# A linear attention followed by an FFT-convolution gate: x2 in row tiles of 128, narrow column tiles, whole q loads with even and odd rows apart, and a new tail

## The chip, the cores and the metric

The kernel runs on one core of a Trainium2 chip, whose engines are TensorE (PE, with its weight loads shown as PEld), VectorE (DVE), ScalarE (ACT), GpSimd (POOL) and SyncE (SP, which here only issues DMAs). The metric is device time in microseconds (us) of one launch. Of the kernel before, three runs took 252.71, 253.55 and 256.71 us; the median is 253.55 us.

## The reference

There are 8 batches, 8 heads, 576 positions (S), 64 features per head (D) and a model width of 512 (DM). Inputs and output are fp32. Attention is linear, with cosine weights on the positions; its output goes through a gate with a circular convolution over the positions.

```
r    = maximum(x, 0);  phi(x) = concat[r * cos(theta), r * sin(theta)]      # theta = pi/2 * pos / S
kv   = phi(k)^T v;  z = sum_s phi(k)
att  = (phi(q) kv) / (phi(q) z + 1e-6)            # per batch and head
x    = att as (batch, S, 512)
x1, x2, x3 = split(x @ w_proj)                    # w_proj: 512 x 1536
conv = irfft(rfft(x2) * rfft(filter_fft))         # along S
out  = (x1 * conv * x3) @ w_out                   # w_out: 512 x 512
```

## The kernel before, in words

All matmul operands are fp16, sums are in fp32. The 576 positions of a batch are held as 6 groups (t or j) of 96 rows. For each batch b the work has these stages; a name in parentheses is the function, the line that of the row in the profile.

- Loads (`load_qk`): q, k and v of a batch are loaded and turned to fp16 by POOL's DMA queue into tiles of 96 partitions, 8 heads and 6 x 64 elements; four buffers serve q, k and v together. From batch 2 on q comes in three DMAs (lines 131 and 133), because the last three groups have even and odd partitions swapped.
- `emit_phi`: phi of k (tile kp) and of q (tile qp), on DVE; lines 102 and 104 are the helper `tsc`.
- `emit_va` (L142): four ACT copies per batch put v into a tile with a constant column beside it.
- `emit_kv` (L527): 48 matmuls per batch, the product of phi(k) and v.
- `emit_qt`: transposes phi(q) to the tile qpt, of which there is one. For batches 0 and 1 TensorE transposes, with the matrices `ident` and `swap`; from batch 2 on SP issues four transposing DMAs (L539), each over two heads, 12 blocks and all 96 partitions.
- `emit_num` (L568): four pieces (hp) of two heads, each 12 matmuls with weights from qpt, read with a stride of two columns; DVE divides (L574, L577) and writes att (L578).
- `emit_xt` (L617): from batch 2 on, one transposing DMA of 24 blocks turns att into xt.
- `emit_fx` (L595, eviction L610 on ACT): folds att along S into 12 groups of 48 columns, that is 6 pairs of real and imaginary parts for three frequency blocks (bl) of 96 rows.
- `emit_x2` (L634, eviction to x2f L639 on ACT): the x2 third of the projection in frequency. For each of the three blocks and two parts, four matmuls with weights of 96 columns and 512 moving columns: 24 per batch.
- `emit_dft` (L649): the rest of the transform, two matmuls for each block, with the tables tre and tim (96 x 96); ACT evicts (L651), DVE multiplies with the filter's transform h3.
- `emit_gate` (L674): the x1 and x3 thirds, 64 matmuls of 288 columns per batch; ACT evicts (L681, L684), DVE multiplies (g, L699).
- `emit_inv` (L710, L711; L714 on ACT) and `emit_y` (L725 to L730 on DVE): the inverse transform, and its product with g, y.
- `emit_out` (L752): y times w_out in five tiles of 128 rows. The five start at rows 0, 128, 256, 384 and 448, so the last repeats 64 rows of the fourth. ACT evicts to os (L759), in groups of tiles (0,1), (2,3), (4); in the last batch DVE does (L102), tile by tile. SP stores the rows (L772), 15 DMAs per batch; in the last batch the odd ones go on ACT's queue, and in the batch before it some on POOL's.

PSUM is one pool of four units with two banks each, which all stages share. The order of the work is written out by hand in the kernel's body and taken up by a scheduler with `behind(mark)`, which holds a piece back until a marked instruction has been issued. In the main loop (b = 1 to 8) x2, dft, gate and inv of batch b are mixed with num and fx of batch b + 1, with phi, qt, va and kv of batch b + 2, and with out of batch b − 1; va and phi of k wait behind marks `x2f` and `att`. SP's queue takes stores, q transposes and xt in the order in which they are issued. A setup phase in the first 60 us computes the tables on DVE, ACT and POOL beside batch 0 and 1. There POOL issues the loads of batch 0, w_proj in three pieces, then q, k and v of batch 1, the filter (`filt`) and w_out (`wo`).

## Time and profile before

| what | value |
|---|---|
| median of three runs | 253.55 us |
| the profiled execution | 253.76 us |
| its span in the profile | 252.0 us |
| mean granted TensorE clock | 0.97 |
| DMA packets, bytes | 74926, 37.30 MB |
| stores of out by SP of 96, 64, 32 KB | 64, 22, 23 |
| q load from batch 2 on, three DMAs each: 288 KB, 144 KB, 144 KB | about 6 us each to landing |
| qpt transposes, issue to landing | 7.1 us |
| xt transposes, issue to landing | 7.7 us |

The profile is one execution. Busy time is the union of an engine's instructions; matmuls overlap in the pipeline, so a single matmul's mean (some 380 ns for 512 columns) is longer than the pitch at which they come. The chain of waits goes back from the last instruction to what released it. A table by windows gives the busy time of each engine in a stretch, its granted clock (1.00 is full) and the DMA's share. Some groups of the page, with busy us, mean ns, idle time before them and its releaser:

```profile
L674 PE MATMUL x<-xt,wp 128*128 128x288 f16 x512 | 68.1, 286 | 0.0
L634 PE MATMUL x<-wp,fx 128*96 128x512 f16 x192 | 48.1, 395 | 1.6 <-DVE qpt L553 1.6
L752 PE MATMUL out<-wo,y 128*128 128x512 f16 x160 | 36.0, 379 | 0.1
L639 ACT ACTIVATE x2f<-x 96x1024 f16<-96x1024 f32 x24 | 24.5, 1020 | 14.2 <-PE x L634 13.9
L142 ACT COPY va<-vraw 96x768 f16<-96x768 f16 x32 | 25.2, 831 | 9.2 <-DMA vraw<-in_v_dram 9.2
```

128*96 is the weights' shape (rows by columns), 128x512 that of the moving operand.

### The profile page before, as it was taken

The numbers are of one execution on the slowest core, as the hardware profiler recorded it, in microseconds if no ns is written. First come the engines' busy times: TensorE is split into PE (matmuls) and PEld (weight loads), VectorE is DVE, ScalarE is ACT, GpSimd is POOL, SyncE is SP. The second block draws the span as 40 slices with busy tenths as digits, with TensorE's granted clock in tenths as the row PEclk, the third lists the DMA queues.
The fourth block names the chain that finished last, engine by engine and source line by source line (L and its number), as shares of the span: only waits on it lengthen the run. The fifth ranks groups of instructions, "written<-read, shape, count | busy, mean of one in ns | idle before, by whom it ended". The sixth has DMA issues, their size and how long they took to land.

```text
span 252.0 us, 6140 instructions
## 1 busy us (share of the span) xinstructions
PE 226.1 (90%) x2313; PEld 159.9 (63%) x2313; DVE 210.4 (83%) x732; ACT 186.2 (74%) x281; POOL 38.1 (15%) x65
## 2 busy tenths in 40 slices
PE   0197897998988999999999999999999999999980
PEld 0067575655676867686768676867686778557730
DVE  7689899699779999999799979997998595828880
ACT  2244789799797876987698769876987488767720
POOL 8714211501501031103110311000000000000030
PEclk9997998899799999999999999999999999999996
DMA  5999999799999969999999999999982512153054
GB/s 68 167 205 205 207 200 153 101 166 196 173 121 157 169 56 202 174 176 194 200 225 143 141 217 199 137 183 156 161 197 53 153 41 58 44 146 83 3 153 140
DMA packets 74926, 37.30 MB, mean 148 GB/s; under 512 B 54288, under 2 KB 70160, under 8 KB 74896
## 3 DMA queue, kind: packets, MB, share of 16 engines
q0 software_dynamic: 26176, 17.21, 51.3%
q1 hardware_dynamic: 48320, 19.11, 40.6%
q10 hardware_dynamic: 400, 0.59, 0.7%
q8 instruction: 18, 0.29, 0.5%
q14 instruction: 12, 0.10, 0.2%
HBM read 33.69 MB, written 9.44 MB: 171 GB/s over the span
## 4 chain that ended last, share of the span: by engine, by line
PE 73%; DVE 13%; ACT 7%; DMA 3%; issue 1%; POOL 1%; POOLq 0%; DVEq 0%; ACTq 0%
PE x L674 21%; PE x L634 17%; PE out L752 12%; PE kv L527 5%; PE num L568 4%; PE fx L595 4%; PE dft L649 3%; DMA vraw<-in_v_dram 3%; PE inv L711 2%; PE inv L710 2%; DVE kp L104 2%; ACT va L142 1%; DVE eo L725 1%; DVE att L578 1%; PE qt L547 1%
## 5 line engine op out<-in xcount | busy, mean ns | idle before, releaser
L674 PE MATMUL x<-xt,wp 128*128 128x288 f16 x512 | 68.1, 286 | 0.0
L674 PEld LDWEIGHTS <-wp 128*128 128x128 f16 x512 | 48.9, 98 | 13.9 <-issue 0.9
L634 PE MATMUL x<-wp,fx 128*96 128x512 f16 x192 | 48.1, 395 | 1.6 <-DVE qpt L553 1.6
L752 PE MATMUL out<-wo,y 128*128 128x512 f16 x160 | 36.0, 379 | 0.1
L639 ACT ACTIVATE x2f<-x 96x1024 f16<-96x1024 f32 x24 | 24.5, 1020 | 14.2 <-PE x L634 13.9
L634 PEld LDWEIGHTS <-fx 128*96 128x96 f16 x192 | 23.0, 127 | 16.7 <-issue 3.7
L142 ACT COPY va<-vraw 96x768 f16<-96x768 f16 x32 | 25.2, 831 | 9.2 <-DMA vraw<-in_v_dram 9.2
L578 DVE TENSOR_TENSOR att<-num,rcp 96x768 f16<-96x768 f32 x32 | 30.3, 948 | 0.2
L752 PEld LDWEIGHTS <-y 128*128 128x128 f16 x160 | 15.3, 97 | 17.7 <-DVE y L730 0.6
L527 PE MATMUL kv<-va,kp 96*128 96x65 f16 x384 | 16.6, 199 | 10.2 <-ACT va L142 8.4
L684 ACT CAST x3s<-x 128x576 f16<-128x576 f32 x32 | 20.5, 641 | 5.9 <-PE x L674 5.9
L759 ACT ACTIVATE os<-out 128x1024 f32<-128x1024 f32 (+1 forms) x21 | 17.7, 880 | 9.0 <-PE out L752 8.7
L610 ACT CAST fx<-fx 128x576 f16<-128x576 f32 x32 | 20.6, 645 | 4.9 <-PE fx L595 4.9
L651 ACT CAST xf<-dft 96x1024 f16<-96x1024 f32 x24 | 24.2, 1008 | 0.0
L527 PEld LDWEIGHTS <-kp 96*128 96x128 f16 x384 | 15.1, 101 | 13.6 <-DVE kp L104 11.3
L699 DVE TENSOR_TENSOR g<-x3s,x1s 128x288 f16<-128x288 f16 x64 | 17.2, 299 | 6.8 <-ACT x3s L684 6.8
L681 ACT CAST x1s<-x 128x576 f16<-128x576 f32 x32 | 20.6, 645 | 1.8 <-PE x L674 0.8
L654 DVE TENSOR_TENSOR m<-xf,h 96x1024 f16<-96x1024 f16 x24 | 16.3, 681 | 6.1 <-ACT xf L651 5.1
L568 PEld LDWEIGHTS <-qpt 128*128 128x128 f16 (+1 forms) x384 | 16.2, 103 | 7.7 <-issue 3.9
L725 DVE TENSOR_TENSOR eo<-eq 128x288 f16<-128x288 f16 x64 | 17.5, 297 | 4.4 <-ACT eq L714 4.4
L595 PE MATMUL fx<-fm,att 96*128 96x96 f16 x240 | 17.0, 214 | 3.4 <-DVE att L578 1.7
L595 PEld LDWEIGHTS <-att 96*128 96x128 f16 x240 | 14.3, 101 | 7.6 <-DVE att L578 3.4
(192 smaller groups left out, 409.1 us busy)
## 6 DMA issues: line engine op xcount, KB each, us to landing
out_dram<-os SPq DMA_DIRECT2D x64, 96.0 KB, 2.2
kraw<-in_k_dram POOLq DMA_DIRECT2D x7, 576.0 KB, 8.6
vraw<-in_v_dram POOLq DMA_DIRECT2D x7, 576.0 KB, 8.9
qraw<-in_q_dram POOLq DMA_DIRECT2D x8, 288.0 KB, 6.0
qraw<-in_q_dram POOLq DMA_DIRECT2D x12, 144.0 KB, 5.9
wp<-in_moe_w_proj_dram POOLq DMA_DIRECT2D x3, 512.0 KB, 11.9
out_dram<-os SPq DMA_DIRECT2D x22, 64.0 KB, 2.2
out_dram<-os SPq DMA_DIRECT2D x23, 32.0 KB, 2.1
```

What stands on the lines that cost most here:

```text
L142: nc.scalar.copy(out=va_buf[b % 2][:, hs, :, 0:D], in_=raw_t[(b, "v")][:, hs].rearrange("p h (j d) -> p h j d", j=NJ),)
L527: nc.tensor.matmul(u[:, h // 4, ds((h % 4) * 65, 65)], kp[:, j, h].rearrange("p a b -> p (a b)"), va[:, h, j, 0:65], start=(j == 0), stop= ...
L568: nc.tensor.matmul(u[0:m, hh, ds(t * 65, 65)], qpt[:, c0 : c0 + 2 * m - 1 : 2], kvs[:, h // 4, ds((h % 4) * 65, 65)], start=True, stop=True,)
L578: mark["att", b, hp] = nc.vector.tensor_tensor(out=att[:, :, ds(hp * 128, 128)].rearrange("p t (h d) -> p h t d", h=2), in0=nv[:, :, :, 0: ...
L595: nc.tensor.matmul(dst.rearrange("p (g e o) -> p g e o", e=2, o=8)[:, :, e], att[:, 2 * j + e, ds(c * 128, 128)], fm[0:NP, gs], start=True ...
L610: mark["fx", b] = nc.scalar.copy(out=dst[:, c].rearrange("p g (j o) -> p j g o", j=3), in_=uf[:, 0:768].rearrange("p (j g o) -> p j g o", ...
L634: nc.tensor.matmul(u[0:NP, comp], fx[:, c, ds(comp * 6 + 2 * bl, 2)].rearrange("p a b -> p (a b)"), wp16[:, c, ds(DM, DM)], start=(c == 0) ...
L639: mark["x2f", b, bl] = nc.scalar.mul(out=x2f[:, bl], in_=u[0:NP], mul=X2SC)
L651: mark["xf", b, bl] = nc.scalar.copy(out=xf, in_=u[0:NP])
L674: nc.tensor.matmul(u[:, hf, 0:HS], wp16[:, i, ds(w * DM + c * 128, 128)], xt[:, i, ds(6 * hf, 6)].rearrange("p a b -> p (a b)") if b < DMA ...
L681: mark["x1s", b, c] = nc.scalar.copy(out=x1s, in_=us[0][:, :, 0:HS])
L752: nc.tensor.matmul(u[:, x], y[:, c, ds(OT[t], 128)], wo16[:, c], start=(c == 0), stop=(c == NC - 1),)
```

## The change

- *q.* q gets a buffer of its own, of 112 partitions, and k and v share three buffers. From batch 2 on q comes in two DMAs: even rows to partitions 0 to 47, odd ones to 64 to 111, each partition's whole 6 x 64 elements at once. phi of q then works on 112 partitions, and qp is laid out by halves of the groups. The transposing DMAs are again four, but each takes 48 partitions and 24 blocks (3 groups of all 8 heads). The positions of att's columns stay what the later stages want; num reads qpt without a stride. Some setup columns (`tcol_m`, `ident`, `swap`, `fm`) are computed for the new order.
- *x2.* fx's 576 columns are taken in four row tiles of 128 and one of 64. The last has its four contracted chunks in two halves, of which one goes to PSUM partitions 0 to 63 and one to 64 to 127, alternating. x2f is 128 partitions by five tiles.
- *dft.* A frequency block now lies across row tiles. Seven padded copies of parts of the tables (tpad) are made in the setup, by seven memsets on DVE and eight DMAs on SP, and three of the six sums take two matmuls, so 9 matmuls instead of 6. The last table has its rows twice, which adds the halves of the fifth tile.
- *out.* The fifth tile is 64 rows. Its 512 columns are computed as two halves of 256, one on PSUM partitions 0 to 63 and one on 64 to 127, in alternating matmuls, evicted as 128 x 256 and stored in two halves per piece. Stores cover 48 rows of one residue; SP issues 17 per batch, and POOL none.
- *va.* From batch 4 on two of the four copies are made on DVE, and the marks that hold them back differ.
- *Order.* In the setup the q load of batch 1, the filter and w_out are issued behind phi(0, q). phi of k waits behind mark `att` 3 instead of 1. In the last batches dft 2 and out of batch 6 come ahead of the gates, inv ahead of the third gate, and out of batch 7 starts with tiles 1 and 0, of which three quarters of the contraction come before the last y is needed; tiles 1 and 0 are evicted by DVE, the others half by DVE and half by ACT, and stores alternate between SP and ACT.

```diff
+    tpad = [consts.tile([128, NP], FP16, tag=f"tpad{i}", name=f"tpad{i}") for i in range(7)]
+    q_buf = consts.tile([112, NH, NJ * D], FP16, tag="qraw", name="qraw")
...
-            nc.gpsimd.dma_start(out=rw[:, hs, 0 : 3 * D], in_=view[:, :, 0 : 3 * D])
-            for x in range(2):
-                nc.gpsimd.dma_start(
-                    out=rw[x::2, hs, 3 * D : 6 * D], in_=view[1 - x :: 2, :, 3 * D : 6 * D]
-                )
+            for e in range(2):
+                nc.gpsimd.dma_start(out=rw[ds(64 * e, 48), hs], in_=view[e::2])
...
+        for i, to, tb, bl, lo, n in (
+            (0, 96, tim, 0, 0, 32), (1, 0, tim, 0, 32, 64), (2, 64, tre, 1, 0, 64),
+            (3, 0, tre, 1, 64, 32), (4, 32, tim, 1, 0, 96), (5, 96, tim, 2, 0, 32),
+            (6, 0, tim, 2, 32, 64), (6, 64, tim, 2, 32, 64),
+        ):
+            nc.sync.dma_start(out=tpad[i][to : to + n], in_=tb[lo : lo + n, bl])
...
+            e, half = hp % 2, hp // 2
             nc.sync.dma_start_transpose(
-                out=qpt[:, hsl].rearrange("p h (j n) -> p (h j) n", j=NJ),
-                in_=qp[:, hsl].rearrange("p h j a b -> p (h j a b)"),
+                out=qpt.rearrange("p h (j e m n) -> p (h j) e m n", j=3, e=2, m=2)[:, :, e, half],
+                in_=qp[ds(64 * ((e + half) % 2), 48), half].rearrange("p h j a b -> p (h j a b)"),
             )
...
-                m = NP if hh and t >= 4 else 128
-                c0 = h * S + 2 * NP * (t // 2) + t % 2
+                m = NP if hh and t == NT - 1 else 128
                 nc.tensor.matmul(
-                    u[0:m, hh, ds(t * 65, 65)], qpt[:, c0 : c0 + 2 * m - 1 : 2],
+                    u[0:m, hh, ds(t * 65, 65)], qpt[:, ds(h * S + t * NP, m)],
...
-            for comp in range(2):
-                for c in range(NC):
-                    nc.tensor.matmul(
-                        u[0:NP, comp],
-                        fx[:, c, ds(comp * 6 + 2 * bl, 2)].rearrange("p a b -> p (a b)"),
-                        wp16[:, c, ds(DM, DM)], start=(c == 0), stop=(c == NC - 1),
-                    )
-            mark["x2f", b, bl] = nc.scalar.mul(out=x2f[:, bl], in_=u[0:NP], mul=X2SC)
+            if bl < 2:
+                for x in range(2):
+                    for c in range(NC):
+                        mm(u[:, x], 2 * bl + x, 128, c, range(NC))
+            else:
+                for c in range(2):
+                    for x in range(2):
+                        mm(u[ds(64 * x, 64), 0], 4, 64, c + 2 * x, range(2 * x, 2 * x + 2))
+            n = 2 if bl < 2 else 1
+            mark["x2f", b, bl] = nc.scalar.mul(
+                out=x2f[:, 2 * bl : 2 * bl + n], in_=u[:, 0:n], mul=X2SC
+            )
...
-            for comp, tab in ((0, tre), (1, tim)):
-                nc.tensor.matmul(u[0:NP, comp], tab[:, bl], x2f[:, bl, comp], start=True, stop=True)
+            for comp in range(2):
+                mm = DFT[2 * bl + comp]
+                for x, (tab, ch) in enumerate(mm):
+                    nc.tensor.matmul(
+                        u[0:NP, comp], tab, x2f[0 : tab.shape[0], ch],
+                        start=(x == 0), stop=(x == len(mm) - 1),
+                    )
...
+    DFT = (
+        ((tre[:, 0], 0),), ((tpad[0], 0), (tpad[1], 1)), ((tpad[2], 1), (tpad[3], 2)),
+        ((tpad[4], 2),), ((tre[:, 2], 3),), ((tpad[5], 3), (tpad[6], 4)),
+    )
...
-    OT = [0, 128, 256, 384, 448]
+    OT = [0, 128, 256, 384, 512]
+    OGL = ((1, 0), (2, 4), (3,))
...
+                if t == 4 and not last:
+                    for c in range(NC):
+                        for hf in range(2):
+                            nc.tensor.matmul(
+                                u[ds(64 * hf, 64), x, 0 : DM // 2], y[:, c, 512:576],
+                                wo16[:, c, ds(hf * (DM // 2), DM // 2)],
+                                start=(c == 0), stop=(c == NC - 1),
+                            )
+                    nc.scalar.mul(
+                        out=os_[t][:, 0, 0 : DM // 2], in_=u[:, x, 0 : DM // 2], mul=OUTSC
+                    )
...
-    load_qk(1, "q")
     load_qk(1, "k")
     load_qk(1, "v")
-    load_filter()
-    load_wo()
...
     emit_phi(0, "q", 4, 4)
+    load_qk(1, "q")
+    load_filter()
+    load_wo()
...
             emit_out(b - 1, OG[0:1])
+            emit_dft(b, (2,))
+            emit_out(b - 1, OG[1:2])
         for c in range(NC):
-            if b == B - 1 and c == NC - 1:
+            if b == B - 1 and c == 2:
                 for x in range(NC):
                     emit_inv(b, x)
...
-            with behind("att", n, 1):
+            with behind(*("att", n, 3)):
                 emit_phi(n + 1, "k")
-            for x in range(2):
-                with behind(*(("x2f", b, x) if b > 1 else ("kvs", 2))):
-                    emit_va(n + 1, (2 * x, 2 * x + 1))
+            if b == 1:
+                with behind("kvs", 2):
+                    emit_va(n + 1)
+            else:
+                with behind("eo", b, 3):
+                    emit_va(n + 1, (0, 1))
+                with behind("g", b, 0):
+                    emit_va(n + 1, (2, 3), nc.vector.tensor_copy)
```

## The prediction, made before the changed kernel ran

> **What bounds the kernel now.** I read the busy shares first, then the slices, the chain of waits, and a table of whole batches.
>
> ```profile
> PE 226.1 (90%) x2313; PEld 159.9 (63%) x2313; DVE 210.4 (83%) x732; ACT 186.2 (74%) x281; POOL 38.1 (15%) x65
> PE   0197897998988999999999999999999999999980
> PE 73%; DVE 13%; ACT 7%; DMA 3%; issue 1%; POOL 1%; POOLq 0%; DVEq 0%; ACTq 0%
> ```
>
> TensorE is busy throughout, except in the first 70 us and the last 20; the chain is 73% PE. Between kv products a batch takes 25.02 us, and PE is busy for all of it. These rows have busy time (count) of PE, PEld, DVE, ACT, POOL:
>
> ```profile
> 94.85:119.87 25.02, 25.02 (x271) 17.99 (x269) 24.25 (x78) 20.79 (x31) 3.65 (x5) 1.00 1.25 186
> 119.87:144.90 25.03, 25.03 (x273) 18.01 (x270) 22.87 (x73) 20.85 (x31) 3.66 (x5) 1.00 1.23 177
> 144.90:169.91 25.01, 25.01 (x271) 17.99 (x268) 22.82 (x73) 20.78 (x31) 1.54 (x2) 1.00 1.21 183
> 169.91:194.93 25.02, 25.02 (x272) 17.98 (x269) 22.25 (x72) 20.79 (x31) 0.00 (x0) 1.00 0.75 143
> ```
>
> So a matmul saved shortens a batch, until DVE (mean 23.05, second) takes over. In the second of these windows DVE waits twice only, 2.0 us together:
>
> ```profile
> DVE rcp L574 <- PE num L568: 1.4, 1, 1.4
> DVE g L699 <- ACT x3s L684: 0.6, 1, 0.6
> ```
>
> The pieces that the change edits, in that batch's chain (start, us):
>
> ```profile
> 121.40 1.74 PE x L634 x8
> ...
> 126.08 0.45 PE dft L649 x2
> ...
> 140.58 4.32 PE out L752 x20
> ```
>
> A 512-column matmul takes 1.74 / 8 = 0.216 us, whether its weights have 128 columns (L752) or 96 (L634); what counts is the number of passes. The weight loads (18 of 25 us) lie beside the matmuls.
>
> **The change part by part.** The sum goes against the profiled execution, 253.76 us (span 252.0 and 1.76 around it), 0.2 above the median 253.55 of the three runs.
>
> *x2.* Today 24 passes of 96 columns, 1.74 + 1.74 + 1.75 = 5.23 us. After: 16 of 128 columns, 3.46 us, and four of 64 that alternate between array columns 0 and 64. Side by side they take 0.43 us, one after another 0.86. So −1.34 or −0.91.
>
> *dft.* Three more passes per batch, as row tiles don't meet the frequency blocks: 3 × 0.216 = +0.65.
>
> *out.* Its fifth tile was four passes of 128 columns, half of them repeated rows. Now 8 passes of 64 × 256, in pairs: 0.43 us, or 0.86 as before. So −0.43 or 0.
>
> *num.* Two of twelve loads had 96 columns, now one; contiguous instead of every second column. In the raw rows passes behind a 96-column load come at 0.045 us, the others at 0.029: some −0.06 for four pieces of a batch.
>
> *Entering and leaving a narrow tile.* The trace has one narrow matmul, L478:
>
> ```profile
> 55.32 0.30 PEld L478 LDWEIGHTS <-alt 96*1 96x1 f16 x3 [0.40 <-issue]
> 56.06 0.12 PEld L649 LDWEIGHTS <-tre 96*96 96x96 f16 x1 [0.44 <-issue]
> ```
>
> The raw rows there give starts 55.014, then 55.323 where the 0.216 pitch calls for 55.23; and 56.061 where it calls for 55.97. So 0.09 us each way. Two narrow groups per batch make 4 × 0.09 = +0.37. Bounds: 0, if it comes from the one-column shape, and 0.09 at every alternation too, 10 more, +0.9. I take 0.37, the row that is nearest.
>
> PE sum per batch: −1.34 + 0.65 − 0.43 − 0.06 + 0.37 = −0.81.
>
> A rule that speaks against the pairs: the Trainium skill's page "TensorE: Matmul & The Clock Gate", part 3 (What overlaps and what doesn't), says weight loads pass in-flight matmuls only where their row groups differ; those of column tiles don't. The gate's 98 ns loads use all rows, as their matmuls do, and still hide under a 0.123 us pitch, so the trace disagrees. By the rule 12 loads of about 0.1 us would show, an estimate of +1.2 per batch; by the row nothing. The same part reports 2.38 times for three column tiles, which no run here shows.
>
> *DVE and ACT.* From batch 4 on, two of four va copies (831 ns each on ACT) move to DVE: 2 × 0.35 (its 96x768 copy, L102) = +0.70 on DVE, −1.66 on ACT. The x2f eviction goes from 3 × 1.02 to 2 × 1.02 + 0.59, −0.43 on ACT. DVE comes to 23.05 + 0.70 = 23.75 of a batch of 24.21, with 0.46 for waits that are 2.0 today. Either they shrink, being slack behind PE, or they stay and the batch is 25.0. I take 0.2 of the 0.81 as not realised, near the first end, since ACT and PE, on which DVE waits, both come earlier: −0.6 per batch.
>
> Six batches (69.8 to 219.79): 6 × −0.6 = −3.6.
>
> *Transposes and queues.* SP now issues xt first, then four q pieces of 24 blocks of 48 rows, where it had four of 12 blocks of 96, with xt between: the same packets. But each new piece holds rows of every head, so the first num needs all four. SP's stores go from 15 to 17 (+2 × 0.4 us issue); no one waits for a store but its buffer. The q load goes from three DMAs to two, and POOL is 15% busy. The loads and q pieces are hidden today by the 25 us of a batch: one batch issues q pieces from 101.99 to 117.8, for a num at 123. I cost them at nothing; the cover is checked as a rival. The skill's "DMA: Bandwidth & Descriptors" (Rules) says that two transfers to disjoint partition halves serialize, so that the split brings nothing; by that the pieces keep today's total, which is also what equal packets give.
>
> *Front.* Between 28 and 42 us the chain is DVE's, and ends in the first x2 (start, us):
>
> ```profile
> 30.59 0.47 DVE qp L102
> ...
> 42.08 0.38 DVE qpt L553
> 42.51 3.52 PE x L634 x8
> ```
>
> The q load of batch 1 moves on POOL's queue from 9.99 behind k1 and v1, and it waits for the single q buffer, about 23. The v1 load, issued there today at 22.23, lands 8.9 us later, 31.1; phi(1,q) starts at 30.5. So DVE stalls some 0.6, and everything queued behind it (kp, g, qpt, and by qpt the first x2) slips. About three small operations more at 0.15: +0.45. The seven memsets fall in a 1.95 us idle at 8.6; ACT gets 0.43 back. I take +0.8, bounds −0.5 (k1 lands sooner) and +2.5 (the load as late as wo's 14 us after its issue). filt and wo also slip, about 1 us; feo starts at 40.8, long after.
>
> *Tail.*
>
> ```profile
> 229.96 3.94 PE x L674 x32
> ...
> 240.67 0.47 DVE y L730
> 241.18 3.86 PE out L752 x17
> 245.06 0.69 DVE os L102
> ```
>
> Before: the last gate, then 0.65 ACT and 6.5 us of DVE, then 17 passes, an eviction, stores, end. After: out(6)'s second group and the last dft go ahead of the gates, which only reorders PE's work, and the inv passes go ahead of the third gate instead of the fourth. Three of the four chunks of tiles 1 and 0 run before the last y, which leaves 20 − 6 = 14 passes × 0.216 = 3.0 us behind it, instead of 3.86. The last eviction (128 x 512 on DVE, 0.69) is cut into a DVE and an ACT half; ACT's rows, 1.024 for 1024 columns and 0.592 for 512, give 0.16 + 0.84 per 1000, so 0.38 for 256; for DVE I put 0.42. So −0.86 − 0.27, and −0.6 for a seventh batch's x2, dft and out: −1.7. Bounds: −0.5, if DVE's chain before the last y hides the seventh saving and ACT's halves come late, and −3, if that chain, before which DVE waits 0.98 us for ACT at 234.64 today, also starts a microsecond earlier, since inv is there earlier. Stores are 19 as before, on the same two queues.
>
> Sum: 253.76 − 3.6 + 0.8 − 1.7 = 249.3.
>
> **Rivals.**
> - *All of it.* No switch price, DVE's waits vanish: −1.18 × 6 = −7.1, front +0.3, tail −2: 245. For it: PE is busy 25.02 of 25.02. Against: L478's 0.09.
> - *DVE becomes the bound.* The waits stay: −0.1 × 6, with front and tail 252.3. For it: DVE 24.25 in one window.
> - *Pairs run one after another.* −0.91 + 0.65 − 0.06 + 0.37 = +0.05 per batch: 253, or 259 if each alternation costs 0.09 as well (+0.93 × 6).
> - *Slower: the q pieces land late.* Place: num(n+1,0), in batches 3 to 7. Four pieces and xt are five transposes of 24 blocks; if each takes SP and DMA 2.85 to 5 us (xt's issue; 4.82 in the batch at 94.85) instead of the piece's best 1.25, they end 5 × 2.85 = 14.3 to 24 us after att is ready at 10 of 25 us. num comes at 27.5. Stalls of 0 to 6.5; at 2 us, 5 × 2 = 10 more: 259. Against: equal packets. It decides against the gain above 4.5 / 5 = 0.9 us per batch, and makes over 2% above 1.9.
>
> **How the numbers follow.** Likeliest 0.38, 249.3, own range 247 to 251.5; all of it 0.22 (243.5 to 246.5); DVE bound 0.13; pairs in turn 0.11; with a price at each alternation 0.04; late q pieces 0.12 (256 to 264). 2%, about what a measurement of this kernel can tell from no change, is 248.5 and 258.6. Faster: 0.22 + a third of 0.38 = 0.35. Slower: 0.04 + 0.12 = 0.16. The rest, 0.49, within. The range 244.5 to 257 leaves out some 0.06 below and 0.13 above.
>
> **What would show it.** Batches between kv products of 24.2 to 24.5, PE busy all of it: right. x2's third group and the fifth out tile taking 0.43 + 0.18 each; 0.86 means one after another. Over 0.5 us of PE idle before num, put down to a DMA: late q pieces. DVE at 24 of a batch with PE idle behind y or att: DVE bound. phi(1,q) later than 30.5: the front. What would make the forecast wrong most: all stalls hidden in the first 70 us, where the trace has waits of every engine and I counted one load.

## The result, and the profile after

The changed kernel takes 270.62 us (median of four runs, 267.8 to 273.04), the kernel before 253.33 (four runs). The ratio is 1.060, with a 95% interval of 1.054 to 1.067; it leaves two of the four runs out as disturbed and so is smaller than the quotient of the medians. The forecast was 249.3, with a range of 244.5 to 257: the time lies outside it, on the other side.

The profiled execution took 268.94 us, its span is 267.2. The page's busy row, the slices of PE and of its granted clock, and the chain's shares:

```profile
PE 220.9 (83%) x2333; PEld 150.4 (56%) x2333; DVE 212.4 (80%) x751; ACT 178.5 (67%) x275; POOL 31.6 (12%) x55
PE   0288977997879999990099985999699999999992
PEclk9999999999999999996579997999999999999999
PE 55%; DMA 20%; ACT 11%; DVE 6%; SPq 4%; issue 1%; POOL 0%; ACTq 0%; POOLq 0%
```

PE has less work than before (220.9 us, not 226.1), and the span is 15 us longer. What is new in the chain is DMA, 20% instead of 3%, and holes in PE's slices after 120, 160 and 187 us. The table by windows, for the batch from 93 us, the hole after it, the 4 us behind the hole, and the next two full batches (busy time and count of PE, PEld, DVE, ACT, POOL; then clock, DMA share, GB/s):

```profile
93.01:117.15 24.14, 24.14 (x273) 17.02 (x272) 23.97 (x75) 19.14 (x29) 3.35 (x4) 1.00 0.82 147
117.15:133.25 16.10, 3.58 (x60) 2.27 (x58) 3.34 (x13) 2.40 (x4) 1.24 (x2) 0.67 1.31 172
133.25:137.34 4.09, 4.09 (x37) 2.48 (x38) 2.52 (x6) 0.00 (x0) 0.00 (x0) 0.62 0.55 157
155.62:186.17 30.55, 26.02 (x273) 17.85 (x272) 23.65 (x75) 19.14 (x29) 2.07 (x3) 0.94 0.88 156
186.17:213.17 27.00, 24.33 (x273) 17.03 (x272) 23.54 (x76) 19.16 (x29) 0.00 (x0) 1.00 0.76 133
```

The first is what was forecast: a batch of 24.14 us, not 25.02, with PE busy for all of it. Then PE does 3.58 us of work in 16.10. What it waits for, from 93 to 213 us:

```profile
PE num L594 <- DMA qpt<-qp: 19.7, 4, 8.0
```

And the chain through the hole (start, us, what):

```profile
113.16 0.83 SPq L564
114.04 2.76 SPq L564
116.85 16.35 DMA qpt<-qp
133.25 1.50 PE num L594 x23
134.74 2.59 PE x L658 x8
137.34 0.38 PE num L594 x12
```

The first num of batch 4 waits for the last transposed q piece, which lands 16.35 us after its issue. When PE resumes, x2's eight passes take 2.59 us instead of 1.73: the granted clock of these stretches is 0.67 and 0.62, not 1.00. What SP and POOL did meanwhile, from the timelines of their queues:

```profile
106.12 3.55 SPq L643 DMA_TRANSPOSE xt<-att  x1
109.77 14.14 SPq L564 DMA_TRANSPOSE qpt<-qp  x4
```

```profile
112.96 1.34 POOL L139 DMA_DIRECT2D vraw<-in_v_dram  x1 [14.54 <-DVE va L144]
116.07 0.77 POOL L139 DMA_DIRECT2D kraw<-in_k_dram  x1 [1.77 <-ACT va L144]
120.78 1.24 POOL L137 DMA_DIRECT2D qraw<-in_q_dram  x2 [3.94 <-DVE qp L107]
```

The four pieces take SP 14.14 us. While they are under way, POOL issues the loads of v, k and q.

It helps to compare the lead, the time from the first piece's issue to the first num, with the time that the pieces need. PE would have come to that num at 120.5 (it idles 7.96 us until 128.47, and 4.56 more until 133.25), so the lead is 10.7 us here; in the next three batches it is 13 to 14. Near the end of the run, where nothing is loaded, the four pieces need 12.7 us from the first issue to the last landing (202.13 to 214.78). In the kernel before, three of the four pieces go out ahead of xt, 17 to 21 us before the first num of their batch, which needs only the first of them. In the batch whose first num starts at 122.98:

```profile
101.99 9.39 SPq L539 DMA_TRANSPOSE qpt<-qp  x3
111.47 4.82 SPq L617 DMA_TRANSPOSE xt<-att  x1
116.38 1.42 SPq L539 DMA_TRANSPOSE qpt<-qp  x1
```

These pieces lay beside loads too (v at 104.37, q at 113.78) and landed up to 11.4 us after their issue, and PE waited for none.

In what follows, "five batches" is the time from the kv product of batch 2 to that of batch 7, from the starts of the kv rows; it leaves the front and the tail out. It is 123.8 us before and 143.7 after.

### The profile page after: what moved, and what is told of

It is laid out like the page before. It is cut to its first block, busy times and chain, and to the rows that moved or that the text cites. A ratio compares the mean times of both kernels' runs of the same rounds, so it can differ in the third digit from the quotient of the medians.

```text
span 267.2 us, 6208 instructions
## 1 busy us (share of the span) xinstructions
PE 220.9 (83%) x2333; PEld 150.4 (56%) x2333; DVE 212.4 (80%) x751; ACT 178.5 (67%) x275; POOL 31.6 (12%) x55
## 4 chain that ended last, share of the span: by engine, by line
PE 55%; DMA 20%; ACT 11%; DVE 6%; SPq 4%; issue 1%; POOL 0%; ACTq 0%; POOLq 0%
PE x L723 22%; DMA qpt<-qp 14%; PE x L658 9%; PE out L795 6%; PE dft L690 5%; SPq L564 4%; PE num L594 3%; DMA qraw<-in_q_dram 3%; ACT va L144 2%; DMA vraw<-in_v_dram 2%; PE fx L621 2%; PE inv L759 2%; PE inv L760 2%; PE kv L550 2%; DVE att L604 1%
## 5 line engine op out<-in xcount | busy, mean ns | idle before, releaser
L676 ACT ACTIVATE x2f<-x 128x1024 f16<-128x1024 f32 (+1 forms) x24 | 21.3, 885 | 40.5 <-PE x L658 40.5
L658 PE MATMUL x<-wp,fx 128*128 128x512 f16 (+1 forms) x160 | 37.4, 396 | 1.7 <-DVE qpt L580 1.0
L594 PE MATMUL num<-kvs,qpt 128*128 128x65 f16 (+1 forms) x384 | 18.2, 201 | 22.2 <-DMA qpt<-qp 19.7
L795 PE MATMUL out<-wo,y 128*128 128x512 f16 (+1 forms) x132 | 30.3, 379 | 0.0
L600 DVE TENSOR_TENSOR rcp<-num,epsc 96x12 f32<-96x12 f32 x32 | 5.1, 160 | 27.6 <-PE num L594 27.6
L144 ACT COPY va<-vraw 96x768 f16<-96x768 f16 x24 | 18.7, 845 | 9.0 <-DMA vraw<-in_v_dram 9.0
L550 PE MATMUL kv<-va,kp 96*128 96x65 f16 x384 | 16.0, 196 | 10.2 <-ACT va L144 8.5
L658 PEld LDWEIGHTS <-fx 128*128 128x128 f16 (+1 forms) x160 | 13.3, 104 | 15.8 <-issue 4.4
L550 PEld LDWEIGHTS <-kp 96*128 96x128 f16 x384 | 14.1, 99 | 13.4 <-DVE kp L107 11.1
L795 PEld LDWEIGHTS <-y 128*128 128x128 f16 (+1 forms) x132 | 12.4, 98 | 14.6 <-issue 0.8
L107 DVE TENSOR_SCALAR kp<-kraw,ccol 96x512 f16<-96x512 f16 (+1 forms) x54 | 18.3, 339 | 1.0 <-DMA kraw<-in_k_dram 1.0
```

The source lines that it names most:

```text
L144: copy(out=va_buf[b % 2][:, hs, :, 0:D], in_=raw_t[(b, "v")][0:NP, hs].rearrange("p h (j d) -> p h j d", j=NJ),)
L550: nc.tensor.matmul(u[:, h // 4, ds((h % 4) * 65, 65)], kp[:, j, h].rearrange("p a b -> p (a b)"), va[:, h, j, 0:65], start=(j == 0), stop= ...
L594: nc.tensor.matmul(u[0:m, hh, ds(t * 65, 65)], qpt[:, ds(h * S + t * NP, m)], kvs[:, h // 4, ds((h % 4) * 65, 65)], start=True, stop=True,)
L658: nc.tensor.matmul(dst, fx[:, c].rearrange("p g o -> p (g o)")[:, ds(128 * ch, n)], wp16[:, c, ds(DM, DM)], start=(c == cs[0]), stop=(c == ...
L676: mark["x2f", b, bl] = nc.scalar.mul(out=x2f[:, 2 * bl : 2 * bl + n], in_=u[:, 0:n], mul=X2SC)
L795: nc.tensor.matmul(us[t], y[:, c, ds(OT[t], nr)], wo16[:, c], start=(c == 0), stop=(c == NC - 1),)
```

## The experiments

Two explanations stood against each other. *Pieces*: the q pieces are late by their own form (24 blocks of 48 rows; all heads in each, so that none can start before the last num and all must be there for the first). *Loads*: the pieces would be in time, if loads of v, k and q didn't run beside them, at times that the three raw buffers and the moved va copies set. A third, that x2, dft, out or the tail cost more than their rows show, had to be excluded.

### e1, e2: the q part undone, and the q part alone

e1 is the changed kernel with the code of before in `load_qk`, `emit_phi`, `emit_qt`, `emit_num` and the setup columns; e2 is the kernel before with the changed ones. The core of e1's edit (e2's is the reverse):

```diff
-    q_buf = consts.tile([112, NH, NJ * D], FP16, tag="qraw", name="qraw")
...
-                out=qpt.rearrange("p h (j e m n) -> p (h j) e m n", j=3, e=2, m=2)[:, :, e, half],
-                in_=qp[ds(64 * ((e + half) % 2), 48), half].rearrange("p h j a b -> p (h j a b)"),
+                out=qpt[:, hsl].rearrange("p h (j n) -> p (h j) n", j=NJ),
+                in_=qp[:, hsl].rearrange("p h j a b -> p (h j a b)"),
```

> The changed kernel with the whole q part undone: loads in three DMAs, four shared raw buffers, phi on 96 partitions, transposing pieces of two heads and 96 rows, strided num, q load of batch 1, filter and w_out issued where they were. x2, dft, out, va and the tail stay as changed. If the q part is the only thing that went wrong (any theory of late pieces), no stall of PE before num is left, batches take 24.2 us, and the time is 244 to 248. If the loads collide because va and the marks moved, which stays here, stalls of 1 to 5 us remain before num and the time is 252 to 262. If x2, out or the tail cost more than their rows show, 254 or more without stalls.

> The kernel before with the q part alone: two q loads, a q buffer of its own, three raw buffers for k and v, 48-row pieces of 24 blocks. x2, dft, out, va and the tail as before. If the form and the release of the pieces make the loss, PE stalls 10 to 20 us before num and the time is 262 to 275. If the moved va copies and their later v load are needed for it, the stalls stay under 3 us and the time is 251 to 257.

e1: 244.73 us against 252.14 before (ratio 0.973, 0.966 to 0.980). Five batches take 120.4, and PE doesn't wait for a piece once. e2: 264.63 (1.050, 1.041 to 1.060), five batches 133.6, with one wait of 8.3 us for the pieces:

```profile
PE num L579 <- DMA qpt<-qp: 8.3, 1, 8.3
```

In e2 the fourth piece still goes out behind xt, as it did before, at 123.26. But now the first num needs it; PE comes to that num at 123.5, and the piece lands at 131.94.

So the q part makes the loss, and everything else in the change is worth 3%. e1 is also the version that beats both kernels. Two of its batches by windows:

```profile
92.62:116.83 24.21, 24.21 (x273) 17.09 (x272) 24.04 (x75) 19.18 (x29) 2.63 (x4) 1.00 1.05 179
116.83:141.04 24.21, 24.21 (x273) 17.09 (x272) 23.55 (x75) 19.18 (x29) 3.55 (x6) 1.00 1.02 178
```

Its SP queue at the place of the hole, with pieces of 12 blocks and 96 rows, again behind xt:

```profile
102.87 2.85 SPq L632 DMA_TRANSPOSE xt<-att  x1
105.82 6.93 SPq L554 DMA_TRANSPOSE qpt<-qp  x4
```

6.93 us instead of 14.14, in the same order and with the same bytes; and POOL's v load comes at 111.98, as late as after (112.96). The trace's DMA rows, counted in stretches of 2 us, show what the difference makes: packets of the transposes that ended, and KB of loads that landed in the same time.

| from | after: packets | after: loads, KB | e1: packets | e1: loads, KB |
|---|---|---|---|---|
| 104 | 0 | 16 | 1487 | 0 |
| 106 | 9 | 4 | 1286 | 0 |
| 108 | 1512 | 0 | 1236 | 0 |
| 110 | 1119 | 0 | 1340 | 0 |
| 112 | 860 | 0 | 1375 | 0 |
| 114 | 909 | 0 | 188 | 126 |
| 116 | 199 | 127 | 0 | 371 |
| 118 | 81 | 334 | 0 | 292 |
| 120 | 442 | 189 | 0 | 279 |
| 122 | 179 | 113 | 0 | 154 |
| 124 | 355 | 230 | 0 | 293 |
| 126 | 336 | 253 | 0 | 185 |
| 128 | 366 | 263 | 0 | 29 |
| 130 | 495 | 178 | 689 | 0 |

The last column's zero at 130 is the end of the burst, and the 689 packets beside it are the next xt's. In this batch of e1 all 6912 packets of xt and the four pieces are through just as the loads begin. After, some 2,500 are left when they begin, and go at 40 to 250 a microsecond until the loads end.

In e1's next two batches the pieces don't get through ahead of the loads. The first of these two, on SP and POOL:

```profile
132.89 8.96 SPq L554 DMA_TRANSPOSE qpt<-qp  x4
136.19 0.77 POOL L139 DMA_DIRECT2D vraw<-in_v_dram  x1 [14.98 <-DVE va L144]
```

The last two pieces land at 144.10 and 147.87, up to 10.2 us after their issue. PE still doesn't wait: num 0 starts at 144.25 and needs the first piece alone, and nums 2 and 3, which need the late ones, start at 146.77 and 147.91. Had each piece held rows of all heads, num 0 would have had to wait for the last, an estimated 3.6 us (147.87 − 144.25). So pieces by heads are covered twice: by the stretch without loads, and by the time from num 0 to num 3.

### e3, e6: twice the blocks, in twice the DMAs

In the kernel before (e3) and in e1 (e6), each piece is cut by rows:

```diff
-            nc.sync.dma_start_transpose(
-                out=qpt[:, hsl].rearrange("p h (j n) -> p (h j) n", j=NJ),
-                in_=qp[:, hsl].rearrange("p h j a b -> p (h j a b)"),
-            )
+            for x, m in ((0, 64), (64, 32)):
+                nc.sync.dma_start_transpose(
+                    out=qpt[:, hsl].rearrange("p h (j n) -> p (h j) n", j=NJ)[:, :, ds(x, m)],
+                    in_=qp[ds(x, m), hsl].rearrange("p h j a b -> p (h j a b)"),
+                )
```

> The kernel before with each transposing piece cut in two by rows, 64 and 32, of the same 12 blocks: the same bytes and packets, twice the blocks, still by heads, so that piece hp starts after num hp and is needed by num hp. If a block costs 0.11 us of the queue whatever its rows, a batch's pieces need 10.6 us instead of 5.3 where nothing else runs; with release by heads kept this is 253 to 258 if order and release matter most, and 262 to 275 if the queue's time alone makes the loss. If equal packets cost the same, pieces stay at 1.3 us for 12 blocks of 96 rows together and the time is 253 to 254.

> The kernel of e1 (old q part, the rest as changed) with each transposing piece cut by rows, 64 and 32: twice the blocks, pieces still by heads, four raw buffers, old loads. If twice the blocks in batches of 24.2 us explain the loss, the last pieces fall into the loads, PE stalls 15 us or more in all before num, and the time is 260 to 272. If a piece over all heads, or the three raw buffers, are needed for it, 245 to 253.

e3: 258.28 (1.027, 1.022 to 1.032), five batches 132.1. e6: 255.14 (1.012, 1.006 to 1.019), five batches 131.0, that is 10.5 us more than e1. Their SP queues say what a block costs. First e6, beside a v load from 110.49 on and late in its run, when nothing is loaded any more; then the changed kernel in such a stretch, then the kernel before:

```profile
104.33 12.59 SPq L555 DMA_TRANSPOSE qpt<-qp  x8
...
190.81 11.63 SPq L555 DMA_TRANSPOSE qpt<-qp  x8
```

```profile
199.22 2.81 SPq L643 DMA_TRANSPOSE xt<-att  x1
202.13 9.60 SPq L564 DMA_TRANSPOSE qpt<-qp  x4
```

```profile
178.74 5.01 SPq L539 DMA_TRANSPOSE qpt<-qp  x3
183.84 3.03 SPq L617 DMA_TRANSPOSE xt<-att  x1
```

Of 96 blocks in all: 12.59 / 96 = 0.13 us a block in e6 (0.12 without loads), 9.60 / 96 = 0.10 after. Of 36 blocks before: 5.01 / 36 = 0.14; e1's 48 take 6.93, again 0.14; xt's 24 blocks 2.81 to 3.03, 0.12. The price follows the blocks and hardly the rows: a piece of 24 blocks takes 2.6 us with 48 rows, xt's 24 blocks of 96 rows 2.8 to 3.0. The same bytes in more blocks therefore take 1.4 times as long after (9.60 against e1's 6.93) and 1.7 to 1.8 times in e6. e6 also has eight DMAs instead of four, each near the floor that e7 shows, so by itself it doesn't tell blocks from DMAs.

In e6 nearly all of the 10.5 us comes in one batch, which takes 33.96 instead of 24.21. PE waits there ahead of nums 1, 2 and 3:

```profile
PE num L584 <- issue: 4.3, 1, 4.3
PE num L584 <- DMA qpt<-qp: 2.9, 2, 2.1
```

The longest of these waits the profile doesn't put down to a piece, but the last one lands at 154.78 and num 3 starts at 154.87. This is somewhat under half of the loss of the changed kernel. It refuted both of the numbers that were expected of it (260 or more; 253 or less).

### e7: the changed pieces by heads

```diff
+            hsl = ds(2 * hp, 2)
+            for e, half in ((0, 0), (1, 0), (0, 1), (1, 1)):
+                nc.sync.dma_start_transpose(
+                    out=qpt[:, hsl].rearrange("p h (j e m n) -> p (h j) e m n", j=3, e=2, m=2)[:, :, e, half],
+                    in_=qp[ds(64 * ((e + half) % 2), 48), half, hsl].rearrange("p h j a b -> p (h j a b)"),
+                )
```

> The changed kernel with its transposing pieces cut by two heads as before, 16 pieces of 6 blocks and 48 rows in a batch: the same number of blocks, but a piece can start after its own num and only the first four are needed by the first num. If it matters that a piece holds all heads, the stalls halve at least and the time is 250 to 260. If only the sum of blocks and the loads beside them count, num 2 or 3 waits instead of num 0 and the time is 265 to 275; more, if each DMA has a price of its own beside its blocks.

293.87 us (1.165, 1.159 to 1.172), five batches 154.9. It didn't test what it was meant to: a transposing DMA has a floor. Sixteen of 6 blocks take SP 21.5 us, 1.3 each, as much as the quickest of 12 blocks.

```profile
115.76 21.53 SPq L565 DMA_TRANSPOSE qpt<-qp  x16
```

### e10: all heads in each piece, with the blocks of before

e10 makes that test with fewer DMAs: e1 with six, one for each of the six groups, 8 blocks of 96 rows each, over all heads. They too are near the floor, but the six take SP little more without loads, 8.0 us (191.81 to 199.84), than e1's four, 6.6 (181.03 to 187.61).

```diff
-            dst[b] = work.tile([NP, NH, NJ, 2, D], FP16, tag="qp", bufs=2, name=f"qp{b}")
+            dst[b] = work.tile([NP, NJ, NH, 2, D], FP16, tag="qp", bufs=2, name=f"qp{b}")
...
+            for x in ((0, 1), (2,), (3, 4), (5,))[hp]:
+                nc.sync.dma_start_transpose(
+                    out=qpt.rearrange("p h (j n) -> p h j n", j=NJ)[:, :, x],
+                    in_=qp[:, x].rearrange("p h a b -> p (h a b)"),
+                )
```

> The kernel of e1 with its pieces cut across the heads: six transposing DMAs of 8 blocks and all 96 rows, one for each of the six groups, so that none can start before the last num of the batch before and all are needed by the first num; 48 blocks as in e1. If pieces over all heads matter by themselves, stalls of 2 us or more come before num 0 and the time is 249 to 258. If the twice as many blocks are what matters, 244 to 247.

259.39 us in the median, with single runs from 251.4 to 263.7 (before: 252.66); no interval can be given. Five batches of the profiled one take 133.6, 13.2 more than e1:

```profile
PE num L584 <- DMA qpt<-qp: 10.7, 4, 5.5
```

So pieces over all heads cost by themselves, though not in every run alike: the profiled run took 258.52, and the quickest, 251.43, is still 6.7 above e1's median. 11.5 of the 13.2 us come in one batch. The trace shows the way. In batch 3 the first piece is issued at 75.0 instead of 72.0, behind the last num; xt at 86.8 instead of 81.9; the stores after it meet the k load, and SP waits in them for earlier stores to land; the next xt goes out at 106.6 instead of 102.9, and the last two pieces (115.5 and 119.4) fall into the loads of 112 to 121. The changed kernel goes the same way: first piece at 75.4, xt at 86.0, the next at 106.1.

### e4: two qpt buffers

```diff
+    qpt_buf.append(late["p"].tile([128, NH * S], FP16, tag="qpt1", name="qpt1"))
...
-            dst[b] = work.tile([112, 2, NH, 3, 2, D], FP16, tag="qp", bufs=2, name=f"qp{b}")
+            dst[b] = work.tile([112, 2, NH, 3, 2, D], FP16, tag="qp", bufs=1, name=f"qp{b}")
```

> The changed kernel with two qpt buffers from batch 3 on (and one qp buffer, to make room), so that the pieces of a batch need not wait until the last num of the batch before has read qpt. If the release is the cause, the pieces go out before or beside xt, the stalls before num go and the time is 245 to 250. If the queue's time or the loads beside it are, the pieces still end late, stalls of 5 us or more remain and the time is 258 to 272.

285.07 us (1.134, 1.125 to 1.143). Inconclusive for the release: the pieces still stand behind xt in SP's order (108.8, after xt at 105.9), and the single qp buffer that made the room set a new wait, 37 us of DVE in phi(q) behind the late pieces, which holds up att and dft.

```profile
DVE qp L105 <- DMA qpt<-qp: 37.0, 3, 13.6
```

### e5, e9: the loads taken away

Both name the raw buffers of k and v by hand; e5 also loads one head of eight for batches 5 to 7.

```diff
-            raw_t[(b, nm)] = q_buf if nm == "q" else work.tile(
-                [NP, NH, NJ * D], FP16, tag="raw", bufs=3, name=f"{nm}raw{b}"
-            )
+            raw_t[(b, nm)] = q_buf if nm == "q" else kv_buf[(2 * b + (nm == "v")) % 3]
         rw = raw_t[(b, nm)]
+        if b >= 5:
+            hs = slice(0, 1)
```

> The changed kernel, with q, k and v of batches 5 to 7 loaded for one head of eight only (the other heads keep an older batch's values; raw buffers are named by hand, in the same turn), so that from 90 us on hardly anything is loaded. If the late pieces come from the loads beside them on the DMA engines, each piece still takes 2.6 us of SP, but the last lands within 6 us, stalls before num are under 1 us and the time is 243 to 249. If SP's time for twice the blocks is enough by itself, stalls of 3 to 6 us before each num remain and the time is 255 to 270.

> The control for e5: the changed kernel with the raw buffers of k and v named by hand, as in e5, and all loads in full. In e5 these named buffers held the start up by 18.7 us (the first num after the setup at 33.1 instead of 14.4), which hid what the loads are worth in its total. If the loads beside the pieces make the stalls, this kernel stalls 10 to 20 us before num after 100 us and takes 272 to 290, against 260 of e5; if they don't, it is within 3 us of e5.

e5: 260.37 us (1.034, 1.028 to 1.040), with a late start (the kv product of batch 2 at 82.5 us instead of 69.5); five batches take 121.2. e9, with all loads: 288.39 (281.2 to 290.3), five batches 150.8. The named buffers change some values of e9's output too, so only its times are read. PE's waits for pieces in the batches from 100 us on, e5 first:

```profile
PE num L595 <- DMA qpt<-qp: 0.9, 1, 0.9
```

```profile
PE num L593 <- DMA qpt<-qp: 26.5, 5, 8.6
```

The pieces of e5 have the changed form, 96 blocks of 48 rows over all heads, and take SP 1.3 to 1.5 us (the first of a batch) and 2.4 to 3.0 (the others). With an eighth of the loads beside them they are in time. Two things limit this pair. The named buffers alone make e9 7 us longer over five batches than the changed kernel. And in the batch from 130 us e5's lead is 14.2 us (119.24 to 133.39), where the changed kernel had 10.7 in its worst batch. The two batches after these compare like with like: the leads are 13.0 and 14.1 us in both kernels, PE's waits 4.5 and 2.7 us in the changed one, 0.9 us and none in e5.

### e15: the loads held back

e15 takes nothing away. One small POOL copy per batch reads a column of each block of qpt, so that POOL issues v, k and q only when the pieces have landed.

```diff
             for x in range(4):
                 emit_qt(n + 1, x)
+            nc.gpsimd.tensor_copy(out=late["gate"], in_=qpt_buf[0][0:1, 0::48])
```

> The changed kernel with one small POOL copy per batch that reads 96 columns of qpt, one in each block, so that POOL issues the next v, k and q loads only when all four pieces have landed. Everything is loaded and computed. If the loads beside the pieces are the cause, the pieces take 2.6 us each and land within 6 us, stalls before num are under 2 us each, and the time is 246 to 253. If the pieces are late by their own length, the stalls stay at 12, 4 and 3 us and the time is 265 to 275; if the held-back loads are late in turn, PE waits before kv or fx and it is 253 to 265.

258.76 us (1.025, 1.018 to 1.031), five batches 133.0. This is some 10 us faster than the changed kernel, and short of the 246 to 253 expected. The chain at the place of the hole:

```profile
115.19 2.57 SPq L564
117.81 6.23 DMA qpt<-qp
124.08 0.91 PE num L594 x23
```

The last piece lands 6.23 us after its issue, not 16.35, and PE waits 1 us. But the loads, now in one burst from 125 us, fall on the next xt, which takes SP 6.73 us instead of 2.9, and the pieces start behind it. The waits that are left:

```profile
PE num L594 <- DMA qpt<-qp: 7.5, 4, 2.2
```

### e11, e12: the raw buffers

e11 is e1 with a q buffer of its own and three raw buffers; e12 the changed kernel with four that are shared.

```diff
-            raw_t[(b, nm)] = q_buf if nm == "q" else work.tile(
-                [NP, NH, NJ * D], FP16, tag="raw", bufs=3, name=f"{nm}raw{b}"
-            )
+            raw_t[(b, nm)] = work.tile([112, NH, NJ * D], FP16, tag="raw", bufs=4, name=f"{nm}raw{b}")
...
+            nc.gpsimd.memset(rw[32:64], 0.0)
```

> The kernel of e1 with a q buffer of its own and three raw buffers for k and v, as in the changed kernel, and its old pieces of 12 blocks. If the buffers move the loads onto the pieces and this is enough, stalls before num of 2 us or more and 249 to 260. If not, 244 to 247.

> The changed kernel with four raw buffers shared by q, k and v, as before, its pieces of 24 blocks kept (POOL also sets 32 rows of each q tile to zero ahead of its load, since the 16 rows between the halves are read). If the buffers, by the turn in which loads are issued, are a needed part of the loss, 250 to 262; if the pieces alone make it, 266 to 275.

e12: 268.56 (1.060, 1.048 to 1.071), five batches 143.3, as the changed kernel. e11: 254.57 (1.009, 1.004 to 1.013), but its start is late (first num of batch 1 at 56.5 instead of 47.2), and it changes some values; five batches take 122.7, 2.3 more than e1, with 2.0 of waiting for pieces. The buffers are no needed part of the loss.

### e13, e14: va as before

```diff
-                with behind("eo", b, 3):
-                    emit_va(n + 1, (0, 1))
-                with behind("g", b, 0):
-                    emit_va(n + 1, (2, 3), nc.vector.tensor_copy)
+                with behind(*(("x2f", b, x) if b > 1 else ("kvs", 2))):
+                    emit_va(n + 1, (2 * x, 2 * x + 1))
```

> The changed kernel with all four va copies on ACT, behind the marks of before, so that v's buffer is free and its load issued some 8 us earlier in a batch. If the v load's turn, right on top of the pieces, is a needed part of the loss, stalls fall to 10 us or less in all and the time is 254 to 264. If not, 266 to 275.

> The kernel of e1 with va as before. No pieces are late there, so only ACT and DVE can tell: 243.5 to 246 if neither sets the end of a batch; 246 to 249 if ACT, with 1.66 us more per batch, holds back evictions that PE waits for, or if the earlier v load meets the stores.

e13, the changed kernel with old va: 266.31 (1.053, 1.045 to 1.062), five batches 140.0. e14, e1 with old va: 248.96 (0.980, 0.973 to 0.986), five batches 124.6. In e14 v is loaded at 101.5, 126.8 and 154.0 and q at 109.4, on top of the pieces, and PE waits 3.6 us for them; in e1 v comes at 112.0 and PE waits for none. So the moved va copies are not what hurts. They keep the time from 104 to 112 us free of loads, which is where the pieces go.

### e8: the narrow passes not alternating

```diff
-                for c in range(2):
-                    for x in range(2):
+                for x in range(2):
+                    for c in range(2):
                         mm(u[ds(64 * x, 64), 0]
...
-                    for c in range(NC):
-                        for hf in range(2):
+                    for hf in range(2):
+                        for c in range(NC):
```

> The kernel of e1 with the narrow passes not alternating: the two of x2's last tile for one array half, then the two for the other, and of out's fifth tile four and four. If pairs run side by side because they alternate, each group takes 0.43 us more or up to that (x2 0.55 to 0.76 or more, out 0.56 to 0.99) and the time is 248 to 251. If the order doesn't matter, 244 to 246.

245.34 us (0.976, 0.969 to 0.982), five batches 120.4, as e1. The groups take the same:

```profile
115.37 0.57 PE out L802 x8
...
123.28 0.56 PE x L647 x4
```

## Why the prediction was wrong, point by point

**The step that failed** is "Transposes and queues": "I cost them at nothing", because of "the same packets". The term was 0; measured, five batches take 143.7 us, 23.2 more than e1's 120.4, and 19.7 of that are PE's waits for the pieces. The packets are the same (6912 a batch with xt), but they don't set the time: 96 blocks of 48 rows take 9.60 us of a queue without loads, 48 of 96 rows 6.93. The kernel before had pieces of 96 rows alone, so its rows couldn't tell a price by blocks from one by packets; equal cost for equal packets was an assumption. The cover that was named, the 25 us of a batch, went with the pieces' form. Before, three of the four went out 17 to 21 us ahead of the first num, and each was needed by its own num. After, all four go out behind the stores and xt, 10.7 to 14 us ahead of the first num, which needs all of them, and 12.7 us is what they need without any load. e1's lead is no longer (11 to 14 us), but its pieces need 9.4 without loads (181.03 to 190.47), and the last is needed 3.6 us after the first. What covers pieces behind xt is thus a stretch of some 10 us between the stores and the next v load, in which nothing is loaded, and, for pieces by heads, the time from num 0 to num 3; e1 uses both up. That the DMA engines were busy stood in the very rows that the prediction shows, in columns that it didn't read: the DMA share is 1.25, 1.23 and 1.21 (it adds up the packets' times, and so can pass 1). By itself it foretells no wait, as PE waited for no piece in those batches.

**The rival** "the q pieces land late" named the place, the reason (24 blocks each, at xt's price) and the condition that all four are needed by the first num. Its price for a piece, 2.85 us, is near the 2.6 of the quiet stretch after 199 us. Its stalls were too small (2 us in each of five batches, against 12.5, 4.5 and 2.7 in three): it went up to 5 us a piece and 6.5 a stall, while the last piece alone landed 16.35 us after its issue. Its chance, 0.12, was given away with "Against: equal packets".

**How far the cause is split.** Against e1's five batches (120.4), twice the blocks cost 10.5 (e6) and all heads in a piece 13.2 (e10, one run of a kernel whose runs differ by 5%); the changed kernel has both and costs 23.2. That the two add up is no proof that they are independent, since each comes mostly from one hole in one batch. With few loads nothing is left (e5), and with loads held back about half (e15, 133.0). So it takes pieces that are longer, or that start late and are needed early, and loads on the same DMA engines. How the loss divides among them in one batch can't be told, as each moves the others. Whether a second qpt buffer would win the early release back was tried only with a side effect (e4) and stays open. Pieces of 96 rows without the swap in the q load were not tried.

**PE's sum was right.** −0.81 per batch was forecast, −0.88 measured (25.02 to 24.14). By the chains' rows: x2 from 5.23 to 1.73 + 1.73 + 0.55 = 4.01, −1.22; dft from 1.31 to 2.09, +0.78; out from 4.32 to 4.02, −0.30; num −0.07; kv, which now follows a narrow tile, 1.53 to 1.63, +0.10; the first gate 2.10 to 1.96, −0.14, which I had not seen; together −0.85. The pairs run side by side: 0.55 for four passes is 0.43 and 0.12 for entering, where 0.18 for both ways had been put; leaving costs 0.10 in kv and 0.12 in dft.

**DVE did not take over.** It is busy 23.97 of 24.14 us with PE never idle. Its waits shrank, as the first of the two ends had it, and the 0.2 us that I left out for it were there.

**Front.** The q load of batch 1 came late as worked out, and the chain shows it:

```profile
23.26 8.38 DMA qraw<-in_q_dram
31.64 0.02 issue
31.66 0.56 DVE qp L105
```

31.64 against a forecast of 31.1. The kv product of batch 1 starts at 45.3, against 45.9 before, which looks like a gain. It isn't one: single profiles differ here. With the loads in the old order kv of batch 1 starts at 41.9 to 44.2 in six kernels (e1, e3, e6, e8, e10, e14), and the profile of the kernel before, 45.9, is the latest of the seven. With the q load moved it starts at 45.3 to 46.8 in seven kernels (the changed one, e2, e4, e7, e12, e13, e15). Between the middle values lie 2.9 us, and 2.2 at kv of batch 2 (68.1 and 70.3). So the front costs about what the upper bound of 2.5 said, not +0.8, as far as single profiles show; how much of it is the q load was not tested apart from the rest of the q part.

**Tail.** From the kv product of batch 7 to the end of the span: 57.2 before, 54.4 in e1. Without one batch's 0.81 that is −2.0, against −1.7.

Taken together, without the pieces: five batches 123.8 to 120.4, −3.4, where 5 × −0.6 = −3.0 was put (the first of them, 23.7 us long before and not 25.02, gained only 0.2); from kv of batch 7 on −2.8, where −0.6 − 1.7 = −2.3 was put; and kv of batch 2 at 69.1 instead of 71.0. In all −8.1, and 252.0 − 8.1 = 243.9 is e1's span. The last −1.9 is no proven gain: e1 has the loads of the setup in the old order, and with that order single profiles reach this point from 66.4 to 71.0.

## What to carry to other kernels

A transfer that is hidden today is hidden by a particular stretch of a particular resource: find the stretch in the DMA rows, and see how full it is, before costing a change of its form at nothing. Price a DMA by a unit that its own rows can tell from the others: 12 blocks in 1.3 us and 24 in 2.85, both of 96 rows, fit blocks, packets and bytes alike, and only a form with other rows decides (24 blocks of 48 rows in 2.6). And a piece that is cut across the consumers, instead of along them, starts with the last release and is needed by the first use.

## What the runs showed of the hardware that was not expected

- A transposing DMA costs SP by its blocks more than by its rows (24 blocks: 2.6 us with 48 rows, 2.8 to 3.0 with 96; 12 blocks of 96 rows: 1.3 to 1.7), with a floor of about 1.2 us (e7, 6 blocks). The Trainium skill's "DMA: Bandwidth & Descriptors" (Rules) says that two transfers to disjoint partition halves bring nothing; for transposes these runs go further, since in parts by rows they take 1.4 times as long (9.60 against 6.93 us, in halves) to 1.8 times (12.59, 64 and 32 rows).
- Transposes beside loads go at 40 to 250 packets a microsecond, alone at 430 to 750 (the table under e1).
- The 64-column passes start in pairs, 3 to 4 ns apart when the program alternates between the halves of the array, and 6 to 14 ns apart when it has the passes of one half first (e8); which pass is which the records don't tell, but x2's four take 0.55 to 0.56 us either way, where one after another they would take 0.86. Their weight loads, 106 to 110 ns, lie beside matmuls. "TensorE: Matmul & The Clock Gate" (part 3, What overlaps and what doesn't) has loads overlap only where row groups differ; here all rows are used by both, and these runs disagree.
- In a pause of PE and for a few us after it the granted clock is lower: 0.67 in the 16.10 us with the hole, 0.62 from 133.25 to 137.34, where x2's eight passes take 2.59 us instead of 1.73. Of the 14.3 us by which the batch from 117 us is longer, 12.5 are waiting; most of the other 1.8 is this (0.86 in x2's passes and some 0.7 in the 23 num passes ahead of them, 1.50 against 0.76 for 24).
